# Packing and decoding sums on VectorE, a second tile for masked scores, and a planner that knows of a shared port

## The chip, the cores and the metric

The kernel runs on one core of one Trainium2 chip. Such a core has TensorE (PE: matrix products, and PEld: its weight loads), VectorE (DVE), ScalarE (ACT), GpSimd (POOL), and SyncE (SP), whose queue issues the kernel's DMA transfers. The metric is the device time of one execution in microseconds (us); lower is better. Before the change three runs gave 865.68, 868.64 and 872.82 us.

## The reference

What is computed is a recurrent attention with a state of 40 x 40 per head, followed by a gated product of two projections:

```python
# r, k, v, w, a, b: batch 4, heads 8, sequence 768, head_dim 40, float32
for t in range(S):
    y[:, :, t] = np.einsum('bhd,bhde->bhe', rt, state)
    Sa = np.einsum('bhde,bhe->bhd', state, at)
    state_decay = state * wt[:, :, None, :] - np.einsum('bhd,bhe->bhde', Sa, bt)
    state = state_decay + np.einsum('bhd,bhe->bhde', vt, kt)
x = y.transpose(0, 2, 1, 3).reshape(B * S, H * D)      # 3072 x 320
out = ((x @ w_a) * (x @ w_b)) @ w_out                  # d_ff = 1536
```

The three weights arrive in 64-bit floating point (a float32 array times a 64-bit scalar), everything else in float32.

## The kernel before

**Tiling.** The sequence is cut into 12 chunks of 64 tokens (n = 0 to 11). Each chunk has two halves of the heads (c = 0, 1), counted together as q = 2n + c, 24 in all. The inner dimension of 1536 is cut into 12 tiles of 128 (f). One *unit* is one tile for one chunk, so there are 144 units.

**Stages of a chunk.** `prep` loads W, BK and A of one q, forms cumulative products with two scans on VectorE (Q and pe), scales BK and A, multiplies them on TensorE into scores, writes one half of the scores to AB and the other, masked, to TK, and stores its results to un_d in DRAM. The rings of W, BK, A, Q and pe have two tiles, TK has one. `lanes` takes a pair of chunks (`GROUPS`): it transposes AB into N, runs 31 steps of two VectorE operations each (Yt, then Y), which invert small triangular matrices, and transposes the result into TC and T3 (the trace calls T3 "T"). `merge` makes the full inverse T from these; for all chunks but the first it copies TC into T by DMA (T<-TC). `main` is the part in which a chunk waits for the one before: the solve (u), the state (s), the outputs (G, y, X). `pack` reads the outputs back as XF, rounds them to a high part xk on ScalarE, and subtracts to get the low part on GpSimd.

**Units.** `decode` turns one piece of 64-bit weights (120 x 384, or 128 x 320 for the output weights) into a high and a low float32 part: five operations on VectorE, some copies on ScalarE, and at last a subtraction (into w_mt) and a sum (into wt or wo) on GpSimd. Three pieces make one tile. A unit multiplies xk by two tiles of wt into ab, forms g = a * b on VectorE and its rounded part gh on ScalarE, subtracts on GpSimd to get gl, and multiplies gh and gl by wo into po. Five tiles (F1) are decoded early and serve chunk 0 to 10 while the recurrence runs; the other seven are decoded at the end of it and during the tail, in which the stored xk of all chunks are read back.

**What sets the order.** All work is given to a planner (`Plan`) as operations with an engine, an estimated duration, dependencies and a priority `v`. `Plan.run` goes through the engines in simulated time: on each it takes, among the operations that can start within 0.05 us of the earliest, the one with the smallest `v`. The code is then emitted in this order, and each engine and the SP queue run their part in order. The priorities are built from PV and PV1 (preparation), LV and LV0 (lanes; LV0 for the first pair), MV (merge), UV (units), WV and WV1 (the first five weight tiles):

```python
prep(n, c, rank[n] + PV + PV1 * (n - rank[n]) + 0.1 * c)
lanes(g, g[0] + LV if g[0] else LV0)
wv = [WV + WV1 * f if f < F1 else NS - 3 + 0.3 * (f - F1) for f in range(NSL)]
```

Nearly all instructions go through a helper in line 68, so that the trace is read by the names of the tiles and not by lines.

Of the kernel before, what the change touches and what calls it, by code (L numbers as in the profile page):

```python
# [9 lines left out]
F32 = mybir.dt.float32  # L10
# [11 lines left out]
D = 40  # L22
C = 64
HB = 32
NP = 2
M = 8
# [47 lines left out]
class Op:  # L74
    __slots__ = ("eng", "dur", "fn", "deps", "users", "v", "lat", "need", "free", "mode", "end", "left", "ready", "seq", "moved", "work")

# [31 lines left out]
class Plan:  # L108
# [8 lines left out]

    def op(self, eng, dur, fn, r=(), w=(), v=None, lat=0.07, need=None, free=(), mode=None, moved=0.0, work=0):
        o = Op()
        o.moved, o.work = moved, work  # L120
# [29 lines left out]
    def run(self, slack=0.05, switch=0.13):  # L150
        engines = {e: 0.0 for e in ("PE", "DVE", "ACT", "POOL", "SP", "-")}
        ring = 0.0
        busy = dict.fromkeys(engines, 0.0)
        last_mode = None
# [10 lines left out]
        while todo:  # L165
            best = None
            for e, ops in ready.items():
                if not ops:
                    continue
                c = []  # L170
                for o in ops:
                    s = max(engines[e], o.ready)
                    if o.need:
                        bk = self.banks(o.need.n, s)
                        if bk is None:
                            continue
# [18 lines left out]
            if o.eng == "PE":  # L195
# [110 lines left out]
def wkv_moe(ctx, tc, wd, ai, bk, rvf, vn, pin, rv, wa, wb, wo, out):  # L306
# [86 lines left out]
    def decode(i, src, rows, ncol, dst_hi, dst_lo, split):  # L393
# [10 lines left out]
        if not WIDE:  # L404
# [53 lines left out]
    def plan_tile(f, w, slot, v):  # L458
        for i, j, (eng, dur, fn, r, wr, lat) in tile_steps(f, w):
# [15 lines left out]
    def unit(xk, kx, w, slot, first, last, done, v):  # L475
# [13 lines left out]
        for j in range(2):  # L489
# [81 lines left out]
    def prep(n, c, v):  # L571
# [12 lines left out]
        pl.op("DVE", us(2 * CW), lambda: nc.vector.tensor_tensor_scan(  # L584
            out=Q[:, CW::-1], data0=W[:, CW::-1], data1=one[:, ::-1], initial=0.0, op0=ALU.mult, op1=ALU.add), [kW], [kQ])
# [6 lines left out]
        eng, dur, te = ("POOL", gp, nc.gpsimd) if n >= ON_POOL else ("DVE", us, nc.vector)  # L592
        pl.op(eng, dur(2 * M * C), lambda: te.tensor_mul(
            out=BK, in0=BK,
            in1=Q[:, 2:2 + CW].rearrange("p (m t) -> p m t", t=CP)[:, :, None, 0:C].to_broadcast([P, M, 2, C])), [kQ], [kBK])
        pl.op("DVE", 0.41, rp, [kQ], ["d1"])

        pl.op("DVE", us(2 * CW), lambda: nc.vector.tensor_tensor_scan(
            out=PEt.rearrange("p m t -> p (m t)"), data0=W[:, 0:CW], data1=D1.rearrange("p m t -> p (m t)"),
            initial=0.0, op0=ALU.mult, op1=ALU.add), [kW, "d1"], [kPE])  # L600
        pl.op(eng, dur(M * C), lambda: te.tensor_mul(out=A, in0=A, in1=PEt[:, :, 0:C]), [kPE], [kA])
        pl.op("ACT", 0.18, lambda: nc.scalar.copy(out=pcs[:, n, c], in_=Qv[:, :, 1]), [kQ], [("pcs", n, c)])
# [67 lines left out]

    def lanes(g, v):

# [13 lines left out]
        pl.op("POOL", 1.2, start, w=["Y"])  # L686
        for s in range(HB - 1):
            ni, w = s + 1, HB - 1 - s

            def step(s=s, ni=ni, w=w):  # L690
                o = Wt[:, 0:ni * w].rearrange("p (i t) -> p i t", i=ni)
                nc.vector.tensor_mul(
                    out=o, in0=Yt[:, 0:ni, s:s + 1].to_broadcast([P, ni, w]),
                    in1=Nt[:, s:s + 1, s + 1:].to_broadcast([P, ni, w]))
                y = Yt[:, 0:ni, s + 1:]
                nc.vector.tensor_sub(out=y, in0=y, in1=o)
            pl.op("DVE", 2 * us(ni * w) + 0.03, step, ["N"], ["Y"])
        pl.op("DVE", 1.95, lambda: nc.vector.transpose(
            out=TC.rearrange("p x m t -> p t (x m)"), in_=Yt.rearrange("p s t -> p t s")), ["Y"], [("TC", 0), ("TC", 1)])
        pl.op("DVE", 1.95, lambda: nc.vector.transpose(  # L700
            out=T3.rearrange("p x m s -> p s (x m)"), in_=Yt), ["Y"], [("T3", 0), ("T3", 1)])

    def merge(n, x, v):
# [56 lines left out]
    def main(n, c, v):  # L760
# [56 lines left out]
        if n < NS - 1:  # L817
# [11 lines left out]
            if n:  # L829
# [6 lines left out]
                out=sv, in0=sv if n else bank(ps)[:, 0:320].rearrange("p (i q d) -> p i q d", q=2, d=D), in1=pc),  # L836
                src + [("pcs", n + 1, c)], [kST], free=[] if n else [(ps, 0)])

# [50 lines left out]
    def pack(n, v):  # L889
# [73 lines left out]
    for g in groups_of_chunks:  # L963
        for n in g:
            prepare(n)
        lanes(g, g[0] + LV if g[0] else LV0)
        if g[0] == 0:
            for f in range(F1):
                plan_tile(f, slots[f], f, wv[f])
        for x, n in enumerate(g):  # L970
            merge(n, x, n + MV)
            prepare(n + 1)
# [3 lines left out]
            if n < NS - 1:  # L976
# [71 lines left out]
    def plan_lazy(f, v):  # L1048
# [12 lines left out]
        for k, (i, j, (eng, dur, fn, r, wr, lat)) in enumerate(tile_steps_at(f, slots[0], base)):  # L1061
# [4 lines left out]
            r = list(r) + ["early"]  # L1066
            pl.op(eng, dur, lambda k=k, steps=steps: steps()[k][2][2](), r, wr, v=v, **kw)
        pl.dma(lambda: fill_rows(slots[slot][0]), [("wt", slot, j) for j in range(2)], [("wf", slot)], 0.3, 1.6, v=v)
# [222 lines left out]
```

## Time and profile before

| | us |
|---|---|
| median of three runs | 868.64 |
| lowest, highest | 865.68, 872.82 |
| the profiled execution | 862.4 |
| its span (first to last instruction) | 860.7 |
| TensorE busy in the span | 705.7 |
| VectorE busy | 581.2 |
| ScalarE busy | 394.6 |
| GpSimd busy | 239.2 |
| mean granted TensorE clock | 0.929 |

The rows of the profile are read so: a group is an engine, an operation, the tiles written and read, the shape and the count, then the busy time in us and the mean of one in ns, then the idle time of the engine just before them with what ended it. A row of waits reads "waiting engine and tile <- what came last: us in total, times, longest". In a timeline the first two numbers are the start and the length in us.

### The profile page before, as it was taken

What the parts mean: (1) busy time and instruction counts of PE and PEld (TensorE: products, weight loads), DVE (VectorE), ACT (ScalarE), POOL (GpSimd) and SP (SyncE); (2) the same over time, 40 slices, a digit from 0 to 9 for tenths busy, and PEclk for the clock granted to TensorE, in tenths of its full rate; (3) what the DMA queues carried; (4) which work ended last, traced back from release to release, by engine and by line L of the source; (5) the groups of instructions that cost most, each with busy time, mean ns of one, the idle gap of its engine ahead of it and who ended that gap; (6) DMA issues with size and microseconds to landing.
All of it is one profiled execution on the core that took longest, in us unless ns stands there. A gap on an engine that the chain in (4) does not pass through costs nothing.

```text
span 860.7 us, 29218 instructions
## 1 busy us (share of the span) xinstructions
PE 705.7 (82%) x12539; PEld 659.9 (77%) x12539; DVE 581.2 (68%) x1121; ACT 394.6 (46%) x1027; POOL 239.2 (28%) x271
## 2 busy tenths in 40 slices
PE   4325666687997898888978889989969999999995
PEld 3324555576887787777867778878969999999995
DVE  8797789999996889687955782256438883223343
ACT  4516553576446644663554435555425542222221
POOL 3000122343321102312220212246526662222221
PEclk9999677669999999999989899999989999999998
DMA  7984788888676968985876566974982210000022
GB/s 245 311 296 123 232 289 240 213 251 259 200 224 192 326 240 267 238 319 190 252 191 212 178 190 177 280 209 124 251 196 64 66 38 1 1 2 1 1 92 97
DMA packets 102019, 156.58 MB, mean 182 GB/s; under 512 B 30250, under 2 KB 70250, under 8 KB 98810
## 3 DMA queue, kind: packets, MB, share of 16 engines
q1 hardware_dynamic: 101882, 154.64, 59.4%
q8 instruction: 100, 1.64, 0.8%
q14 instruction: 37, 0.30, 0.1%
HBM read 101.97 MB, written 48.78 MB: 175 GB/s over the span
## 4 chain that ended last, share of the span: by engine, by line
PE 42%; DVE 27%; DMA 17%; issue 6%; ACT 4%; SPq 2%; POOL 1%; DVEq 0%; ACTq 0%; POOLq 0%
PE ab L68 20%; PE at L68 12%; PE po L68 10%; DVE Yt L68 6%; DVE Y L68 6%; DMA BK<-in_bk_dram 3%; DMA xk<-xk_d 2%; DMA wraw<-in_wa_dram 2%; SPq L68 2%; DVE w_ex L68 2%; DMA W<-in_wd_dram 2%; DVE BK L68 2%; DVE G L68 2%; DMA SV<-in_vn_dram 2%; DVE Q L68 1%
## 5 line engine op out<-in xcount | busy, mean ns | idle before, releaser
L68 PE MATMUL ab<-xk,wt 120*128 120x256 f32 x2304 | 316.1, 290 | 1.8 <-DVE g L68 1.0
L68 PEld LDWEIGHTS ab<-xk,wt 120*128 120x128 f32 x2304 | 297.9, 196 | 4.4 <-DVE g L68 1.2
L68 POOL TENSOR_TENSOR gl<-g,gh 128x256 fp32r<-128x256 f32 x144 | 118.3, 823 | 394.1 <-ACT gh L68 370.6
L68 DVE TENSOR_TENSOR g<-ab,g 128x256 f32<-128x256 f32 x144 | 60.5, 421 | 174.3 <-ACT g L68 173.9
L68 PE MATMUL po<-wo,gh 128*128 128x320 f32 x576 | 156.5, 321 | 10.9 <-ACT gh L68 8.7
L68 ACT COPY g<-ab 128x256 f32<-128x256 f32 x144 | 53.4, 371 | 144.8 <-PE ab L68 140.4
L68 PEld LDWEIGHTS po<-wo,gh 128*128 128x128 f32 x576 | 104.8, 193 | 13.3 <-ACT gh L68 9.8
L68 PE MATMUL po<-wo,gl 128*128 128x320 f32 x288 | 93.4, 324 | 6.9 <-POOL gl L68 6.8
L68 ACT CAST gh<-g 128x256 fp32r<-128x256 f32 x144 | 58.2, 405 | 66.9 <-DVE g L68 64.5
L68 DVE TENSOR_TENSOR Y<-Y,Yt 128x31 f32<-128x31 f32 (+15 forms) x186 | 73.0, 393 | 6.4
L68 DVE TENSOR_TENSOR Yt<-Y,N 128x31 f32<-128x31 f32 (+15 forms) x186 | 73.7, 396 | 4.9
L68 PE MATMUL at<-SV,un 128*64 128x40 f32 (+1 forms) x1472 | 50.9, 230 | 25.2 <-DMA SV<-in_vn_dram 10.2
L68 PEld LDWEIGHTS at<-SV,un 128*64 128x64 f32 (+1 forms) x1472 | 45.0, 141 | 31.6 <-issue 17.4
L68 PE MATMUL at<-ident,BK 128*128 128x128 f32 x192 | 39.0, 364 | 36.7 <-ACT AB L68 16.3
L68 PEld LDWEIGHTS po<-wo,gl 128*128 128x128 f32 x288 | 55.7, 194 | 12.0 <-POOL gl L68 11.4
L68 PEld LDWEIGHTS at<-ident,BK 128*128 128x128 f32 x192 | 30.2, 187 | 40.5 <-ACT AB L68 21.0
L68 POOL TENSOR_TENSOR w_mt<-w_mt,wt 120x384 f32<-120x384 f32 x24 | 26.2, 1090 | 93.8 <-ACT wt L68 74.0
L68 PE MATMUL at<-A,BK 64*64 64x64 f32 x1536 | 36.2, 258 | 13.3 <-ACT bkn L68 6.3
L68 PEld LDWEIGHTS at<-A,BK 64*64 64x64 f32 x1536 | 32.3, 168 | 18.2 <-ACT bkn L68 8.8
L68 DVE TENSOR_TENSOR BK<-BK,Q 128x1024 f32<-128x1024 f32 x24 | 30.9, 1286 | 21.0 <-DMA BK<-in_bk_dram 20.8
L68 DVE TENSOR_TENSOR acc<-po,acc 128x320 f32<-128x320 f32 x96 | 42.4, 481 | 3.1 <-PE po L68 2.5
L68 POOL TENSOR_TENSOR xk<-XF,xk 120x512 fp32r<-120x512 f32 (+1 forms) x24 | 33.2, 1405 | 37.5 <-ACT xk L68 37.5
(87 smaller groups left out, 1100.6 us busy)
## 6 DMA issues: line engine op xcount, KB each, us to landing
un<-un_d SPq DMA_DIRECT2D x24, 1092.0 KB
BK<-in_bk_dram SPq DMA_DIRECT2D x24, 512.0 KB
rv<-in_rvf_dram SPq DMA_DIRECT2D x24, 512.0 KB
xk_d<-xk SPq DMA_DIRECT2D x11, 720.0 KB
xk<-xk_d SPq DMA_DIRECT2D x11, 720.0 KB
un_d<-bkn SPq DMA_DIRECT2D x24, 320.0 KB
SV<-in_vn_dram SPq DMA_DIRECT2D x24, 320.0 KB
W<-in_wd_dram SPq DMA_DIRECT2D x24, 260.5 KB
```

Source lines behind the costliest of these rows:

```text
L68: r = fn(*args, **kwargs)
```

## The change

1. **Packing.** With `PACK_DVE = 12` the two subtractions of `pack` run on VectorE for all 12 chunks, in place of GpSimd.
2. **Decoding.** With `DEC_DVE = 15` the last subtraction and the sum of `decode` run on VectorE for the pieces 0 to 14, the five early tiles. Later pieces stay on GpSimd.
3. **gl.** The unit's subtraction gets the same switch, but `GL_DVE = 0` leaves it on GpSimd for every unit.
4. **TK.** `NTK = 2` gives the masked scores a second tile.
5. **The planner.** An operation can now hold a port. A GpSimd operation (all but the clearing of Y) and a marked VectorE operation may not overlap in the planned order: either waits for the end of the other engine's last one. Marked are the lane steps, the scans and products of `prep`, decoding, packing, and one product of `main`.
6. **Priorities.** All nine numbers change, for instance PV from -2.5 to -3.09, LV0 from -2.6 to -0.99, WV from 1.0 to -1.
7. **Not in use.** A way to halve the lanes (`HALVED`, `join`) is added, and `HALVED = ()` leaves it out. `ON_POOL`, which was 99 and never reached, is removed.

```diff
-NTK, NBN = 1, 1
+NTK, NBN = 2, 1
-ON_POOL = 99
+GL_DVE, PACK_DVE, DEC_DVE = 0, 12, 15
+HALVED = ()
-PV, PV1, LV, MV, UV, WV, WV1 = -2.5, 0.4, -0.6, -0.2, 1.6, 1.0, 0.3
-LV0 = -2.6
+PV, PV1, LV, MV, UV, WV, WV1 = -3.09, 0.6, -0.62, -0.34, 1.28, -1, 0.88
+LV0 = -0.99
...
+        o.moved, o.work, o.port = moved, work, port or (eng == "POOL" and dur != 1.2)
...
+        port = {"DVE": 0.0, "POOL": 0.0}
...
                     s = max(engines[e], o.ready)
+                    if o.port:
+                        s = max(s, port["DVE" if e == "POOL" else "POOL"])
...
+            if o.port:
+                port[o.eng] = s + d
...
-        yield "POOL", us(ncol, 0.2, 0.0027), lambda: nc.gpsimd.tensor_sub(
+        eng, d, te = ("DVE", us(ncol), nc.vector) if i < DEC_DVE else ("POOL", us(ncol, 0.2, 0.0022), nc.gpsimd)
+        yield eng, d, lambda: te.tensor_sub(
             out=shaped(f), in0=shaped(f), in1=dst_hi.bitcast(F32)), (kd + (0,),), (K[1],), None
-        yield "POOL", us(ncol, 0.2, 0.0027), lambda: nc.gpsimd.tensor_add(
+        yield eng, d, lambda: te.tensor_add(
             out=dst_lo, in0=shaped(f), in1=shaped(rf)), (K[1], K[2]), (kd + (1,),), None
...
-        pl.op("POOL", 0.76, lambda: nc.gpsimd.tensor_sub(out=gl, in0=g, in1=gh.bitcast(F32)),
-              [("g", i), ("gh", i)], [("gl", i)], v=v - 0.4)
+        eng, d, te = ("DVE", 0.43, nc.vector) if nunit <= GL_DVE else ("POOL", 0.76, nc.gpsimd)
+        pl.op(eng, d, lambda: te.tensor_sub(out=gl, in0=g, in1=gh.bitcast(F32)),
+              [("g", i), ("gh", i)], [("gl", i)], v=v - 0.4, port=True)
...
-        pl.op("POOL", 1.3, lambda: nc.gpsimd.tensor_sub(out=xk[:, 3:5], in0=XF[:, 0:2], in1=xf[:, 0:2]), kf + [k + (0,)], [k + (1,)], v=v)
+        eng, d, te = ("DVE", 0.7, nc.vector) if n < PACK_DVE else ("POOL", 1.38, nc.gpsimd)
+        pl.op(eng, d, lambda: te.tensor_sub(out=xk[:, 3:5], in0=XF[:, 0:2], in1=xf[:, 0:2]), kf + [k + (0,)], [k + (1,)], v=v, port=True)
...
-        pl.op("POOL", 1.3, lambda: nc.gpsimd.tensor_sub(
-            out=xk[0:D, 2:6:3], in0=XF[0:D, 2:4], in1=xf[0:D, 2:6:3]), kf, [k + (2,)], v=v)
+        pl.op(eng, d, lambda: te.tensor_sub(
+            out=xk[0:D, 2:6:3], in0=XF[0:D, 2:4], in1=xf[0:D, 2:6:3]), kf, [k + (2,)], v=v, port=True)
```

**GpSimd, before the first units.** w_mt, wt and wo are pieces of the second weight tile, xk the packing of chunk 0, gl and Y the units' subtraction and the clearing for the next lanes. Before:

```order
L68 TENSOR_TENSOR w_mt0_167<-w_mt0_167,wt1_231 120x384
L68 TENSOR_TENSOR wt1_231<-w_mt0_167,w_rs0_168 120x384
L68 TENSOR_TENSOR w_mt0_167<-w_mt0_167,wo1_232 128x320
L68 TENSOR_TENSOR wo1_232<-w_mt0_167,w_rs0_168 128x320
L68 TENSOR_TENSOR xk0_220<-XF_219,xk0_220 120x512
L68 TENSOR_TENSOR xk0_220<-XF_219,xk0_220 40x2x256
L68 TENSOR_TENSOR gl0_173<-g0_169,gh0_171 128x256
L68 TENSOR_TENSOR gl1_174<-g1_170,gh1_172 128x256
```

and now, from the clearing for the second pair on:

```order
L70 MEMSET Y_198 128x1024
L70 MEMSET Y_198 128x32
L70 TENSOR_TENSOR gl0_173<-g0_169,gh0_171 128x256
L70 TENSOR_TENSOR gl1_174<-g1_170,gh1_172 128x256
L70 TENSOR_TENSOR gl0_173<-g0_169,gh0_171 128x256
```

Decoding and packing have left this queue; gl and the clearing of Y remain.

**VectorE, at the first pair's lanes.** N is the transposed AB, Yt and Y the lane steps, the names with w_ the decoding. Before:

```order
L68 SCALAR_TENSOR_TENSOR Q0_183<-W0_181,one_81 128x521
L68 TENSOR_TENSOR TK0_191<-at2_65,tri_84 128x512
L68 STREAM_TRANSPOSE N_196<-AB_195 128x32x32
L68 TENSOR_TENSOR Yt_198<-Y_197,N_196 128x31
L68 TENSOR_TENSOR Y_197<-Y_197,Yt_198 128x31
L68 TENSOR_TENSOR Yt_198<-Y_197,N_196 128x60
```

and now:

```order
L70 STREAM_TRANSPOSE N_197<-AB_196 128x32x32
L70 SCALAR_TENSOR_TENSOR w_ex0_166<-wraw1_165,w_ex0_166 120x384
L70 TENSOR_TENSOR BK0_187<-BK0_187,Q0_183 128x1024
L70 TENSOR_TENSOR A0_189<-A0_189,pe0_193 128x512
L70 TENSOR_TENSOR w_mt0_167<-w_ex0_166,w_mt0_167 120x384
L70 TENSOR_TENSOR w_rs0_168<-w_rs0_168,w_ex0_166 120x384
L70 TENSOR_SCALAR w_ex0_166<-wraw0_164 128x320
L70 TENSOR_TENSOR w_mt0_167<-w_mt0_167,wt0_230 120x384
L70 TENSOR_TENSOR wt0_230<-w_mt0_167,w_rs0_168 120x384
L70 TENSOR_TENSOR TK0_191<-at1_64,tri_84 128x512
```

The steps used to follow the transpose at once; four more operations of decoding stand after these rows before the first of them.

**SP, at the inverses of the third pair.** T0 and T1 are the copies for chunk 4 and 5, which wait for the lanes; un_d12 is what the preparation of q = 12 stores, and so on. Before:

```order
L68 DMA T0_204<-TC_199 32x16x32 x4
L68 DMA T1_205<-TC_199 32x16x32 x4
L68 DMA un_d12_143<-pe0_192 128x520
L68 DMA un_d12_143<-A0_189 64x2x256 x2
L68 DMA un_d12_143<-bkn0_194 128x640
L68 DMA xk_d3_98<-xk1_221 120x1536
L68 DMA BK0_187<-in_bk_dram 128x1024
L68 DMA W0_181<-in_wd_dram 128x521
```

and now:

```order
L70 DMA T0_205<-TC_200 32x16x32 x4
L70 DMA T1_206<-TC_200 32x16x32 x4
L70 DMA xk_d3_98<-xk1_222 120x1536
L70 DMA un_d14_145<-pe0_193 128x520
L70 DMA un_d14_145<-bkn0_195 128x640
L70 DMA un_d14_145<-A0_189 64x2x256 x2
L70 DMA BK0_187<-in_bk_dram 128x1024
L70 DMA W0_181<-in_wd_dram 128x521
```

The loads of W and BK behind the copies are those of q = 14 before, and of q = 16 now: two rounds of preparation have moved ahead of them.

More of the change, by code (lines that the diff above doesn't have):

```diff
@@ L24 @@
 HB = 32
+QB = 16
 NP = 2
@@ L74 @@
 class Op:
-    __slots__ = ("eng", "dur", "fn", "deps", "users", "v", "lat", "need", "free", "mode", "end", "left", "ready", "seq", "moved", "work")
+    __slots__ = ("eng", "dur", "fn", "deps", "users", "v", "lat", "need", "free", "mode", "end", "left", "ready", "seq", "moved", "work", "port")
 class Banks:
@@ L356, in wkv_moe @@
             base=0, channel_multiplier=-1)
+    if HALVED:
+        off = const.tile([P, HB], F32, name="off")
+        nc.gpsimd.memset(off, 0.0)
+        nc.gpsimd.memset(off[:, QB:], -1.0)
+        eye = const.tile([P, HB], F32R, name="eye")
+        for qd in range(4):
+            sl = off[qd * HB:(qd + 1) * HB, :]
+            nc.gpsimd.affine_select(
+                out=sl, in_=sl, pattern=[[0, HB]], compare_op=ALU.is_ge, fill=0.0,
+                base=QB - 1, channel_multiplier=-1)
+            nc.scalar.copy(out=eye[qd * HB:(qd + 1) * HB, :], in_=ident[qd * HB:(qd + 1) * HB, qd * HB:(qd + 1) * HB])
     bias = const.tile([P, 1], F32, name="bias")
@@ L669, in prep, with lanes @@
         pl.op("ACT", 1.6, size, [kPE, kQ], [kW], v=v + 0.5)
-    def lanes(g, v):
+    def lanes(g, v, halved):
         pl.v = v
@@ L686, in lanes, with step, part @@
         pl.op("POOL", 1.2, start, w=["Y"])
[L687 to L697, printed above, removed]
+        if halved:
+            off_ = [AB[:, x0 + x, :, 0:HB] for x in range(len(g))]
+            for x in range(len(g)):
+                pl.op("DVE", us(512), lambda x=x: nc.vector.tensor_mul(
+                    out=off_[x], in0=off_[x], in1=off[:, None, :].to_broadcast([P, NP * M, HB])),
+                    ["N"], [("EO", x0 + x)] + kab, port=True)
+            for s in range(QB - 1):
+                ni, w = s + 1, QB - 1 - s
+                def step(s=s, ni=ni, w=w):
+                    def part(t, i0, n, t0, w):
+                        a = t[:, i0:i0 + 1, t0:t0 + 1]
+                        return bass.AP(tensor=a.tensor, offset=a.offset, ap=[a.ap[0], [QB * HB + QB, 2], [HB, n], [1, w]])
+                    o = Wt[:, 0:2 * ni * w].rearrange("p (b i t) -> p b i t", b=2, i=ni)
+                    nc.vector.tensor_mul(
+                        out=o, in0=part(Yt, 0, ni, s, 1).to_broadcast([P, 2, ni, w]),
+                        in1=part(Nt, s, 1, s + 1, w).to_broadcast([P, 2, ni, w]))
+                    y = part(Yt, 0, ni, s + 1, w)
+                    nc.vector.tensor_sub(out=y, in0=y, in1=o)
+                pl.op("DVE", 2 * us(2 * ni * w) + 0.03, step, ["N"], ["Y"], port=True)
+        else:
+            for s in range(HB - 1):
+                ni, w = s + 1, HB - 1 - s
+                def step(s=s, ni=ni, w=w):
+                    o = Wt[:, 0:ni * w].rearrange("p (i t) -> p i t", i=ni)
+                    nc.vector.tensor_mul(
+                        out=o, in0=Yt[:, 0:ni, s:s + 1].to_broadcast([P, ni, w]),
+                        in1=Nt[:, s:s + 1, s + 1:].to_broadcast([P, ni, w]))
+                    y = Yt[:, 0:ni, s + 1:]
+                    nc.vector.tensor_sub(out=y, in0=y, in1=o)
+                pl.op("DVE", 2 * us(ni * w) + 0.03, step, ["N"], ["Y"], port=True)
@@ L701, in lanes, with join, xt, t3 @@
             out=T3.rearrange("p x m s -> p s (x m)"), in_=Yt), ["Y"], [("T3", 0), ("T3", 1)])
+    def join(n, x, v):
+        pl.v = v
+        EO, XT = AB[:, place[n]], W4
+        ps = Banks(1)
+        def xt(ps=ps):
+            mul(bank(ps).rearrange("p (m t) -> p m t", t=HB), fl, eye[:, None, :].to_broadcast([P, NP * M, HB]), True, False)
+            for cm in range(NP * M):
+                for q in range(4):
+                    r = slice(q * HB, (q + 1) * HB)
+                    mul(bank(ps)[r, cm * HB:(cm + 1) * HB], EO[r, cm, 0:HB], T3[r, x, cm], False, True)
+        pl.op("PE", 2.55, xt, [("EO", place[n]), ("T3", x)], [("j1", n), "W4"], need=ps, work=3072, mode="h", lat=0.1)
+        pl.op("ACT", act(512), lambda ps=ps: nc.scalar.copy(
+            out=XT, in_=bank(ps).rearrange("p (m t) -> p m t", t=HB)), [("j1", n)], ["W4"], free=[(ps, 0)])
+        ps, ps2 = Banks(1), Banks(1)
+        def t3(ps=ps):
+            for cm in range(NP * M):
+                for h in range(2):
+                    r = slice(C * h, C * h + HB)
+                    mul(bank(ps)[r, cm * HB:(cm + 1) * HB], TC[r, x, cm], XT[r, cm])
+        def tc_(ps=ps2):
+            for cm in range(NP * M):
+                for q in range(4):
+                    r = slice(q * HB, (q + 1) * HB)
+                    mul(bank(ps)[r, cm * HB:(cm + 1) * HB], XT[r, cm], TC[r, x, cm])
+        pl.op("PE", 1.15, t3, ["W4", ("TC", x)], [("j2", n), ("T3", x)], need=ps, work=1024, mode="h", lat=0.1)
+        def t3c(ps=ps):
+            for h in range(2):
+                r = slice(C * h, C * h + HB)
+                nc.scalar.copy(out=T3[r, x], in_=bank(ps)[r].rearrange("p (m t) -> p m t", t=HB))
+        pl.op("ACT", 2 * act(512), t3c, [("j2", n)], [("T3", x)], free=[(ps, 0)])
+        pl.op("PE", 2.3, tc_, ["W4", ("j2", n)], [("j3", n), ("TC", x)], need=ps2, work=2048, mode="h", lat=0.1)
+        pl.op("ACT", act(512), lambda ps=ps2: nc.scalar.copy(
+            out=TC[:, x], in_=bank(ps).rearrange("p (m t) -> p m t", t=HB)), [("j3", n)], [("TC", x)], free=[(ps2, 0)])
     def merge(n, x, v):
@@ L965, in wkv_moe @@
             prepare(n)
-        lanes(g, g[0] + LV if g[0] else LV0)
+        halved = groups_of_chunks.index(g) in HALVED
+        lanes(g, g[0] + LV if g[0] else LV0, halved)
         if g[0] == 0:
@@ L970, in wkv_moe @@
         for x, n in enumerate(g):
+            if halved:
+                join(n, x, n + MV)
             merge(n, x, n + MV)
@@ L1066, in plan_lazy @@
             r = list(r) + ["early"]
-            pl.op(eng, dur, lambda k=k, steps=steps: steps()[k][2][2](), r, wr, v=v, **kw)
+            pl.op(eng, dur, lambda k=k, steps=steps: steps()[k][2][2](), r, wr, v=v, port=eng == "DVE", **kw)
         pl.dma(lambda: fill_rows(slots[slot][0]), [("wt", slot, j) for j in range(2)], [("wf", slot)], 0.3, 1.6, v=v)
```

22 lines of the change are left out of this document (10 added, 12 removed).

## The prediction

> **What bounds the kernel now.** I read the page's busy shares and slices first, then the chain of waits, then a table of stages.
>
> ```profile
> span 860.7 us, 29218 instructions
> ...
> PE 705.7 (82%) x12539; PEld 659.9 (77%) x12539; DVE 581.2 (68%) x1121; ACT 394.6 (46%) x1027; POOL 239.2 (28%) x271
> ...
> PE   4325666687997898888978889989969999999995
> DVE  8797789999996889687955782256438883223343
> ...
> PE 42%; DVE 27%; DMA 17%; issue 6%; ACT 4%; SPq 2%; POOL 1%; DVEq 0%; ACTq 0%; POOLq 0%
> ```
>
> TensorE (PE) is full only in the right third. To the left VectorE (DVE) is the fuller engine, and the chain runs through both. The stages are cut where each pair of chunks has its triangular inverses ready, at the six transposes into T3 (called T in the trace):
>
> ```profile
> L68 DVE STREAM_TRANSPOSE T<-Y x6: 1969/1993/2071, 70.0 to 512.4; 128x1024 f32<-128x1024 f32 x6
> ...
> core 0: us, PE busy (x) PEld busy (x) DVE busy (x) ACT busy (x) POOL busy (x), PEclk, DMA share, GB/s
> 0.00:70.04 70.04, 24.60 (x425) 20.48 (x425) 58.54 (x112) 24.07 (x63) 10.03 (x23) 1.00 0.78 262
> 70.04:155.69 85.65, 56.84 (x1526) 51.02 (x1526) 71.07 (x139) 44.67 (x115) 14.92 (x15) 0.78 0.80 241
> 155.69:251.45 95.76, 79.04 (x1711) 71.25 (x1712) 90.33 (x166) 54.94 (x141) 33.95 (x34) 0.84 0.77 231
> 251.45:340.82 89.37, 76.77 (x1878) 69.40 (x1877) 73.45 (x135) 49.72 (x136) 15.52 (x16) 0.94 0.78 245
> 340.82:425.13 84.31, 73.61 (x1740) 66.36 (x1740) 66.80 (x130) 45.82 (x127) 17.84 (x16) 0.94 0.80 252
> 425.13:512.40 87.27, 70.83 (x1770) 64.51 (x1768) 60.80 (x119) 41.23 (x111) 16.09 (x15) 0.90 0.66 196
> 512.40:600.00 87.60, 79.34 (x1604) 74.74 (x1602) 40.04 (x75) 46.57 (x118) 32.60 (x34) 0.98 0.70 196
> 600.00:652.00 52.00, 44.86 (x336) 43.82 (x335) 24.57 (x46) 18.79 (x46) 22.93 (x27) 0.93 0.82 205
> 652.00:860.70 208.70, 199.82 (x1565) 198.36 (x1563) 95.58 (x209) 68.82 (x172) 75.34 (x93) 0.99 0.11 36
> ```
>
> Columns two to six are the stage's length and the busy times of PE, its weight loads, DVE, ACT and POOL. The reader is to see that the pace of the first three stages is VectorE's: 90.33 of 95.76 us in the third. In the next three neither engine is full (PE idles 12.6, 10.7 and 16.4 us, VectorE 15.9, 17.5 and 26.5): they wait for each other and for loads. From 512 us on the inverses are done. By the order of the instructions TensorE has 50 of 144 expert units behind it when it begins the last chunk's solve, before and after, so what follows is the same work. Whatever shifts 512.4 us shifts the end.
>
> **The work that moves.** To 512.4 us POOL ran these:
>
> ```profile
> L68 POOL TENSOR_TENSOR gl<-g,gh 128x256 fp32r<-128x256 f32 x40 | 37.9, 950 | 221.9 <-ACT gh L68 200.5 <-issue 19.8 <-DVE w_rs L68 1.6
> L68 POOL TENSOR_TENSOR xk<-XF,xk 120x512 fp32r<-120x512 f32 (+1 forms) x18 | 25.4, 1435 | 25.9 <-ACT xk L68 25.9
> L68 POOL TENSOR_TENSOR wt<-w_mt,w_rs 120x384 fp32r<-120x384 f32 x10 | 12.9, 1285 | 1.1 <-DVE w_rs L68 0.6
> L68 POOL TENSOR_TENSOR w_mt<-w_mt,wt 120x384 f32<-120x384 f32 x10 | 10.9, 1095 | 79.3 <-ACT wt L68 62.1 <-DVE Q L68 5.3 <-DVE Yt L68 4.4
> L68 POOL TENSOR_TENSOR wo<-w_mt,w_rs 128x320 fp32r<-128x320 f32 x5 | 4.5, 903 | 0.4
> L68 POOL TENSOR_TENSOR w_mt<-w_mt,wo 128x320 f32<-128x320 f32 x5 | 4.3, 864 | 28.7 <-ACT wo L68 28.7
> ```
>
> The gl row stays (GL_DVE is 0), and the halved lanes and `join` are not used (HALVED is empty). The 18 packing and 30 decoding subtractions and sums go to VectorE. Its price for such shapes (minimum/median/maximum, ns):
>
> ```profile
> L68 DVE TENSOR_TENSOR A<-A,pe x24: 653/689/1602, 7.8 to 455.5; 128x512 f32<-128x512 f32 x24
> ...
> L68 DVE TENSOR_TENSOR w_rs<-w_rs,w_ex x36: 475/548/2574, 40.4 to 706.0; 120x384 f32<-120x384 f32 x24, 128x320 f32<-128x320 f32 x12
> ...
> L68 DVE TENSOR_TENSOR_SCAN Q<-W,one x24: 1215/1243/2678, 3.8 to 433.7; 128x521 f32<-128x521 f32 x24
> ```
>
> 18 x 0.689 + 20 x 0.548 + 10 x 0.475 = 12.4 + 11.0 + 4.7 = **28.1 us more on VectorE**. The same rows show what comes back: maxima are two to five times the median. Such records have a POOL operation beside them (the columns are the start and the length in us):
>
> ```profile
> 90.29 2.04 DVE L68 TENSOR_TENSOR_SCAN Q<-W,one 128x521 f32<-128x521 f32 x1
> ...
> 139.86 0.42 DVE L68 TENSOR_TENSOR Y<-Y,Yt 128x247 f32<-128x247 f32 x1
> 140.31 1.50 DVE L68 TENSOR_TENSOR Yt<-Y,N 128x240 f32<-128x240 f32 x1
> 141.85 1.37 DVE L68 TENSOR_TENSOR Y<-Y,Yt 128x240 f32<-128x240 f32 x1
> ...
> 140.26 2.70 POOL L68 TENSOR_TENSOR xk<-XF,xk 120x512 fp32r<-120x512 f32 x2 [9.00 <-ACT xk L68]
> ...
> 490.61 1.40 DVE L68 TENSOR_TENSOR Y<-Y,Yt 128x256 f32<-128x256 f32 x1
> ```
>
> Two lane steps that should take 0.41 us take 1.50 and 1.37 while POOL packs. Between the 90.29 and the 490.61 record, 35 records of VectorE are longer than the usual one of their shape and lie mostly beside a packing or decoding operation; together they are 28.8 us too long. So **28.8 us come back**, and the two terms nearly cancel. Bounds of the return: 28.8 if the neighbour was the cause, nothing if others take its place. I take the whole, since each of the 35 has its operation beside it.
>
> The Trainium skill (SBUF — State Buffer, section "SBUF: two separate sides") has the port of these two engines as an exclusive lock, held for a whole instruction. By that rule the return is whole, as the rows have it; a port that was merely shared would return about half, 14.4 us, and the sum below would be 871.6.
>
> **Order and second TK tile.** The rest is in the order: new numbers for the priorities, and a planner that keeps the two engines apart. Three places matter.
>
> Loads for preparation. SP's queue runs in order, and the copy T<-TC waits there for the inverses. Before, 14 of the 24 loads of W and of BK stand ahead of it in the third pair; afterwards 16, and in the fifth 24 of each instead of 24 and 22. So the next pair's loads no longer begin behind that wait. What VectorE and TensorE wait for there, 250 to 600 us:
>
> ```profile
> DVE BK L68 <- DMA BK<-in_bk_dram: 11.0, 4, 4.9
> DVE Q L68 <- DMA W<-in_wd_dram: 6.5, 3, 2.9
> DVE TK L68 <- DMA un_d<-TK: 2.2, 1, 2.2
> ...
> PE po L68 <- POOL gl L68: 5.0, 7, 1.4
> ```
>
> 11.0 + 6.5 = 17.5 us could go; the other end is 0, because the queue's DMA share is 0.66 to 0.80 in those stages and a load moved ahead can hold up another. I take half, **8.7 us**. The second TK tile by itself is worth 0 to 2.2 us (one wait in the run) and is counted in that half: with it a pair's scores need not wait until the former TK has been stored.
>
> POOL's queue. A gl behind two packings waits some 2.8 us; TensorE waits 5.0 us for gl in seven places. Gain 0 to 5.0; I take **2**, since some of the seven are gl held by VectorE.
>
> The ramp. Between the transpose into N and the first lane step of the first pair VectorE now has 13 operations, ten of decoding and three of preparation: some 7.5 us, if the ten take the 0.475 to 0.548 of w_rs and the three the 0.689 to 1.243 of A and Q. Two of the weight loads also stand ahead of the fourth load of BK in SP's queue. All of this has to be done anyway, and the first weights are ready sooner: by the order three units instead of one stand before the third chunk's solve. TensorE idles 28.8 us in the second stage, where that can be used. Bounds +7.5 and -5; I take 0, as the two are alike in size.
>
> The tail from 600 us keeps its decoding on POOL (pieces 15 and up). One load of output weights slides behind the reloads of xk; it can repeat this stall once more, 0 to 6.3 us; I take 0, TensorE has a queue of units there.
>
> ```profile
> 642.79 0.63 PE L68 MATMUL po<-wo,gh 128*128 128x320 f32 x1 [6.31 <-ACT gh L68]
> ```
>
> **Sum.** The profiled execution took 862.4 us (span 860.7 and 1.7 around it). 862.4 + 28.1 - 28.8 - 8.7 - 2.0 = 851.0, a gain of 11.4 us. The median of the runs, 868.64, lies 6.2 us above that execution; carried over to it: 868.6 - 11.4 = **857.2 us**.
>
> **Rivals.**
> *More than that:* the waits of the fourth to sixth stage go and TensorE sets the pace. It idles 39.7 us there; half of it, 19.9, and the 2 of gl make 846.7. For it: VectorE's 59.9 idle us there. Against it: the waits lie on several releasers, and a solve, a state and the next solve depend on each other.
> *The order does nothing:* the loads are paced by their rings of two and by the DMA share, and come as late as now. Then only 0.7 and 2.0 go: 865.9. For it the share of 0.8 in the early stages, against it the loads that now stand ahead of the wait.
> *Slower, by a packing that heads VectorE's queue:* on POOL a packing may wait for its rows at no cost (25.9 us in the row above). On VectorE all lane steps queue behind it, and TensorE's next solve behind them. The copy ahead of it waits for its rows:
>
> ```profile
> ACT xk L68 <- DMA XF<-x_d: 7.5, 6, 2.6
> ```
>
> 7.5 us is the least by which packings would be late, 25.9 the most by these rows. With 25.9 the time is 857.2 + 25.9 = 883.1. It decides from 20.1 us on, where the time passes 877.3. Against it: the planner sets the packing where it expects the rows.
> *Slower, by a full VectorE:* nothing of the 28.8 comes back, because lanes now meet gl where they met packings. 857.2 + 28.8 = 886.0. For it gl's 40 operations of 950 ns that stay, against it the 35 records with another neighbour. The Trainium skill (Perfetto Trace Analysis, section "Optimizing Scalar/DVE Operations") would hand work from a saturated VectorE to others, the reverse of this change, and adds that between these two engines that may not help, for the port.
>
> **How the numbers follow.** About 1% (8.7 us) is what a measurement of this kernel tells from no change. Forecast 0.45, with a range of its own of 848 to 866, two thirds of it under 860; more than that 0.15; the order does nothing 0.18; the packing in front 0.14; a full VectorE 0.08. Faster by over 1%: 0.30 + 0.15 = 0.45. Within 1%: 0.15 + 0.18 = 0.33. Slower: 0.22. The forecast's own range is its sum with the loads' term at 0 and at 17.5. The range goes from 843, which leaves out a third of the larger gain, to 882, which leaves out the upper half of both slower cases: 0.05 and 0.11.
>
> **What would show it.** Right: VectorE's scans and lane steps near their medians wherever POOL runs no gl; VectorE's busy time to the last T3 within 5 us of 421; waits for BK and W after 250 us under 9 us; the last T3 at 495 to 508 us. Wrong: idle time of VectorE ahead of xk operations (packing in front), gl rising above 1.1 us with lane steps lengthened as often as now (full VectorE), or the last T3 at 512 with waits for BK and W as long as before (the order does nothing).

## The result and the profile after

| kernel | median of its runs | kernel before beside it | ratio, 95% interval |
|---|---|---|---|
| changed, first time | 837.8 us (4 runs, 834.5 to 844.5) | 869.3 us (4 runs) | 0.9648 [0.9575, 0.9720] |
| changed, measured again | 840.3 us (6 runs, 836.2 to 852.5) | 864.7 us (17 runs, 856.6 to 880.4) | 0.9728 [0.9676, 0.9779] |

Medians are of all runs of a kernel, while a ratio compares only the runs within 1.5% of the fastest of their kernel, so it need not be the quotient of two medians.

The change is faster by 24 to 31 us. The prediction said faster, with 857.2 us and a range that began at 843. It was right in direction, but the time is 17 to 19 us below its forecast and 3 to 5 us below its range, and the gain of 11.4 us that it named is less than half of the measured one.

The first profile of the changed kernel is its slowest run (844.5 us, span 842.8). The readings below are from the second one (836.2 us, span 834.5), which lies 4 us below its median, as the profile of before (862.4) lies 2 to 7 us below its own. The page of that second profile, busy shares, slices and chain:

```profile
span 834.5 us, 29196 instructions
...
PE 691.6 (83%) x12539; PEld 651.0 (78%) x12539; DVE 569.3 (68%) x1175; ACT 396.7 (48%) x1027; POOL 167.0 (20%) x217
...
PE   4332758658899888988897999979979999999996
...
DVE  8789888898989767887886884266347765232343
...
PE 53%; DMA 17%; DVE 8%; ACT 6%; issue 4%; SPq 1%; POOL 1%; ACTq 0%; DVEq 0%; POOLq 0%
```

VectorE (DVE) fell from 27% of the chain to 8%, TensorE (PE) rose from 42% to 53%. TensorE's idle time, span less busy time, went from 155.0 to 142.9 us, and its busy time from 705.7 to 691.6 for the same 12539 products. So more than half of the 26.2 us between these two spans is shorter busy time, and why the same products took less was not tried. The stages, cut as before at the six transposes into T3:

```profile
L70 DVE STREAM_TRANSPOSE T<-Y x6: 1852/1988/2020, 75.7 to 502.1; 128x1024 f32<-128x1024 f32 x6
```

(in the first profile they run from 75.8 to 508.8 us)

```profile
0.00:75.74 75.74, 23.23 (x425) 19.88 (x425) 61.82 (x124) 25.62 (x63) 7.17 (x21) 0.61 0.78 249
75.74:172.43 96.69, 64.95 (x1658) 58.13 (x1658) 83.92 (x173) 54.73 (x140) 3.76 (x5) 0.75 0.80 253
172.43:265.91 93.48, 80.23 (x1794) 73.35 (x1795) 83.40 (x173) 53.74 (x140) 9.53 (x12) 0.86 0.77 242
265.91:353.30 87.39, 75.92 (x1812) 69.99 (x1811) 66.72 (x133) 46.58 (x127) 10.60 (x13) 0.90 0.78 244
353.30:431.32 78.02, 68.62 (x1801) 62.77 (x1800) 64.76 (x131) 46.10 (x125) 8.31 (x11) 1.00 0.84 268
431.32:502.12 70.80, 63.50 (x1610) 58.17 (x1609) 55.92 (x117) 37.72 (x103) 8.03 (x11) 0.95 0.68 207
502.12:590.00 87.88, 82.83 (x1634) 77.32 (x1633) 43.09 (x89) 47.71 (x122) 28.46 (x33) 1.00 0.76 214
590.00:642.00 52.00, 47.31 (x363) 47.10 (x362) 26.87 (x57) 21.50 (x52) 22.31 (x28) 0.97 0.64 161
642.00:834.50 192.50, 185.00 (x1455) 184.28 (x1454) 82.79 (x188) 62.98 (x156) 68.86 (x85) 0.99 0.10 34
```

The second stage is 11 us longer than it was (96.69 against 85.65), the fifth 6 us and the sixth 16 us shorter. The last T3 comes 10.3 us sooner, at 502.1 instead of 512.4, and **what follows it takes 332.4 us instead of 348.3**. In the last three rows TensorE is busy for 315.1 us with 3452 products, where it was 324.0 us with 3505, and idle for 17.2 us instead of 24.3. In the first profile the last T3 comes 3.6 us sooner and what follows takes 334.0 us. The stages end at other amounts of work, though, so they do not say alone where time was gained. For that the next rows cut both kernels where TensorE had done equal work, each product weighted by the mean time of its group; their numbers in brackets are nearly the same. First the kernel before:

```profile
413.88:546.67 132.79, 114.00 (x2756) 104.44 (x2754) 81.77 (x162) 63.42 (x171) 24.08 (x25) 0.94 0.70 207
546.67:673.33 126.66, 112.51 (x1322) 108.63 (x1320) 72.47 (x136) 59.68 (x145) 61.57 (x67) 0.96 0.67 174
```

Then the changed kernel:

```profile
410.60:528.20 117.60, 109.74 (x2779) 101.22 (x2776) 85.71 (x182) 63.18 (x173) 13.95 (x19) 0.97 0.73 224
528.20:648.50 120.30, 111.12 (x1321) 107.41 (x1322) 62.87 (x133) 57.14 (x139) 51.30 (x59) 0.99 0.68 185
```

259.5 us became 237.9: **21.6 of the 26.2 us between the two spans lie in this stretch**. TensorE idles 17.0 us there instead of 32.9, and its busy time is 5.7 us less, with a granted clock of 0.97 and 0.99 instead of 0.94 and 0.96. Up to 413.9 us only 3.3 us had been gained, and the tail from 648.5 us takes 186.0 us against 187.4.

The waits of VectorE on loads and of TensorE on gl, 250 to 600 us:

```profile
DVE Q L70 <- DMA W<-in_wd_dram: 5.4, 2, 3.2
...
DVE BK L70 <- DMA BK<-in_bk_dram: 2.2, 2, 1.3
```

```profile
PE po L70 <- POOL gl L70: 1.1, 3, 0.5
```

17.5 us of waits for W and BK became 7.6, 5.0 us for gl became 1.1, and the 2.2 us for the store of TK are gone. How far such sums vary by themselves is seen in experiment 9.

### The profile page after: what moved, and what is told of

It is laid out like the page before. It is cut to its first block, busy times and chain, and to the rows that moved or that the text cites. A ratio compares the mean times of both kernels' runs of the same rounds, so it can differ in the third digit from the quotient of the medians.

```text
span 842.8 us, 29196 instructions
## 1 busy us (share of the span) xinstructions
PE 690.6 (82%) x12539; PEld 650.2 (77%) x12539; DVE 570.4 (68%) x1175; ACT 396.2 (47%) x1027; POOL 167.4 (20%) x217
## 4 chain that ended last, share of the span: by engine, by line
PE 53%; DMA 22%; DVE 10%; ACT 6%; issue 5%; SPq 2%; POOL 1%; ACTq 0%; DVEq 0%; POOLq 0%
PE ab L70 25%; PE at L70 16%; PE po L70 12%; DMA SV<-in_vn_dram 6%; DMA XF<-x_d 3%; DMA x_d<-X 3%; DMA wraw<-in_wo_dram 2%; DVE Yt L70 2%; DVE Y L70 2%; DMA acc<-po_d 2%; SPq L70 2%; DMA wraw<-in_wa_dram 2%; DMA un_d<-A 2%; ACT SV L70 1%; DMA un_d<-bkn 1%
## 5 line engine op out<-in xcount | busy, mean ns | idle before, releaser
L70 PE MATMUL ab<-xk,wt 120*128 120x256 f32 x2304 | 311.3, 288 | 9.1 <-DVE g L70 8.3
L70 PEld LDWEIGHTS ab<-xk,wt 120*128 120x128 f32 x2304 | 294.5, 194 | 12.6 <-DVE g L70 8.7
L70 POOL TENSOR_TENSOR gl<-g,gh 128x256 fp32r<-128x256 f32 x144 | 113.9, 793 | 537.6 <-ACT gh L70 535.0
L70 DVE TENSOR_TENSOR Y<-Y,Yt 128x31 f32<-128x31 f32 (+15 forms) x186 | 65.4, 352 | 6.4
L70 DVE TENSOR_TENSOR Yt<-Y,N 128x31 f32<-128x31 f32 (+15 forms) x186 | 64.6, 347 | 4.6
L70 PE MATMUL at<-ident,BK 128*128 128x128 f32 x192 | 33.7, 324 | 19.2 <-DVE TK L70 7.0
L70 ACT COPY SV<-ST 64x160 f32<-64x160 f32 x88 | 28.5, 323 | 37.6 <-DMA SV<-in_vn_dram 35.1
L70 PEld LDWEIGHTS at<-ident,BK 128*128 128x128 f32 x192 | 25.7, 165 | 22.8 <-DVE TK L70 7.9
L70 ACT COPY SV<-at 64x160 f32<-64x160 f32 x96 | 27.5, 287 | 25.3 <-PE at L70 24.0
L70 PE MATMUL at<-T,AB 32*32 32x32 f32 x768 | 17.0, 204 | 25.3 <-DVE T L70 23.1
```

What stands on the lines that cost most here:

```text
L70: r = fn(*args, **kwargs)
```

## The experiments

Each ratio is to runs of the kernel before on the same chip. "Old order" is that of the kernel before and "new order" that of the changed one, instruction by instruction on every engine.

### 1. The sums on VectorE, the old order

```diff
-lambda: nc.gpsimd.tensor_sub(out=shaped(f), ...)
+lambda: (nc.vector if i < 15 else nc.gpsimd).tensor_sub(out=shaped(f), ...)
...
-lambda: nc.gpsimd.tensor_sub(out=xk[:, 3:5], ...)
+lambda: nc.vector.tensor_sub(out=xk[:, 3:5], ...)
```

(and the same for the sum of decoding and the second subtraction of packing)

> The order of the kernel before, with nothing changed in its planner or numbers; only the packing of all pairs of chunks and the decoding sums of pieces 0 to 14 are issued on VectorE instead of GpSimd (POOL), at the places where the old order has them relative to their inputs. Placement theory (the gain lies in where the sums run, because a POOL operation holds up VectorE): 838 to 850 us, and the records of VectorE to the last T3 fall back to their medians. Order theory (the sums cancel, 28.1 against 28.8, and the numbers and the port in the planner make the gain): 862 to 875 us. If the sums, at places planned for POOL, head VectorE's queue: above 875 us.

870.4 us (10 runs), ratio 0.9993 [0.9943, 1.0044]: no change. VectorE to the last T3 at 513.5 us, in a row of windows, and its moved groups there:

```profile
0.00:513.50 513.50, 384.72 (x9042) 345.68 (x9042) 416.16 (x843) 260.51 (x693) 47.33 (x71) 0.89 0.76 235
```

```profile
L68 DVE TENSOR_TENSOR xk<-XF,xk 120x512 fp32r<-120x512 f32 (+1 forms) x18 | 12.7, 706 | 7.1 <-ACT xk L68 7.0
...
L68 DVE TENSOR_TENSOR w_mt<-w_mt,wt 120x384 f32<-120x384 f32 x10 | 5.4, 543 | 0.7 <-ACT wt L68 0.7
L68 DVE TENSOR_TENSOR wt<-w_mt,w_rs 120x384 fp32r<-120x384 f32 x10 | 5.4, 542 | 0.0
...
L68 DVE TENSOR_TENSOR w_mt<-w_mt,wo 128x320 f32<-128x320 f32 x5 | 2.4, 482 | 0.9 <-ACT wo L68 0.9
L68 DVE TENSOR_TENSOR wo<-w_mt,w_rs 128x320 fp32r<-128x320 f32 x5 | 2.4, 480 | 0.0
```

The five groups add 28.3 us, yet VectorE's busy time fell from 421.0 to 416.2, so 33.1 us came back. Counted record by record up to the last T3, those more than 0.25 us over the median of their shape were 53 in the kernel before, 37.4 us too long together, and are 20 here, 9.1 us too long. The 20 lie beside gl or the clearing of Y, which stay on GpSimd. That is what the placement theory wanted to see, and still the time stood. In the old order placement alone is not the gain.

### 2. The sums on POOL, the new order

```diff
-eng, d, lambda: te.tensor_sub(out=shaped(f), ...)
+eng, d, lambda: nc.gpsimd.tensor_sub(out=shaped(f), ...)
```

(and the same for the other three)

> The changed kernel's order, but the packing and the decoding sums are issued on POOL at the same places. Placement theory: the lengthened records of VectorE come back beside them, 855 to 875 us. Order theory: the sums cancel here too, 832 to 846 us. A mixture would lie between, 846 to 855 us.

845.0 us (4 runs), ratio 0.9750 [0.9676, 0.9825], within the order theory's numbers. Against 0.9648 and 0.9728 the sums' place would be worth 0.2 to 1.0% here, 2 to 9 us, but the interval holds 0.9728, so that it is worth anything by itself is not shown.

### 3 and 4. The priority numbers

```diff
-PV, PV1, LV, MV, UV, WV, WV1 = -3.09, 0.6, -0.62, -0.34, 1.28, -1, 0.88
-LV0 = -0.99
+PV, PV1, LV, MV, UV, WV, WV1 = -2.5, 0.4, -0.6, -0.2, 1.6, 1.0, 0.3
+LV0 = -2.6
```

The first of the two is the changed kernel with this edit, the second the kernel before with its reverse. (The numbers are eight, as the diff has them; the texts on record speak of nine.)

> The changed kernel with the nine old priority numbers; the placement of the sums, the port in the planner and the second TK tile stay as changed. If the numbers make the gain: 860 to 875 us. If placement and port make it: 832 to 848 us. If the numbers were merely fitted to the placement, so that neither stands alone: 848 to 860 us.

> The kernel before with the nine new priority numbers and nothing else. If the numbers make the gain: 832 to 848 us. If placement and port make it: 862 to 880 us, since the numbers then only shift work whose limits stay as they were.

866.4 us, ratio 1.0013 [0.9964, 1.0062], and 862.0 us, ratio 0.9947 [0.9898, 0.9995]. The old numbers lose the whole gain, and the new ones alone bring 0.5%. Each result by itself points at the other half, so neither half alone makes the gain. The second kernel also speaks on a premise of the prediction; its row is shown with that of the next.

### 5. The planner without the port

```diff
-o.moved, o.work, o.port = moved, work, port or (eng == "POOL" and dur != 1.2)
+o.moved, o.work, o.port = moved, work, False
```

> The changed kernel, its planner no longer keeping VectorE and POOL apart; the sums stay on VectorE. If keeping them apart makes the gain: 850 to 870 us, with records of VectorE lengthened beside gl. If the lengthened records are not what costs (the sums already left POOL, only gl and the tail's decoding remain there): 835 to 845 us.

858.4 us, ratio 0.9880 [0.9802, 0.9958]: 1.5 to 2.3% lost. The records of VectorE beside gl did lengthen, as the first theory has it, but by little: 21 records up to the last T3 are more than 0.25 us over the median of their shape, 9.5 us together, where the changed kernel has 10 and 4.7 us. So most of the 13 to 20 us lies in the other order that the planner makes. The last T3 of experiment 4, and of this kernel:

```profile
L68 DVE STREAM_TRANSPOSE T<-Y x6: 1874/1982/2047, 74.8 to 495.4; 128x1024 f32<-128x1024 f32 x6
```

```profile
0.00:491.13 491.13, 365.92 (x8753) 331.85 (x8753) 414.04 (x833) 256.84 (x677) 47.17 (x71) 0.90 0.77 241
```

The second row is the window up to that kernel's last T3. The two reach it at 495.4 and 491.1 us, before the changed kernel (502.1 and 508.8), and end later (spans 857.4 and 856.1). In the latter TensorE has 8753 products behind it at that point, in the six stages of the changed kernel some 9100, so 365.0 us follow where the changed kernel has 332.4. So the last T3 by itself doesn't set the end. What TensorE has done by then counts as much.

### 6. Rounded numbers

```diff
-PV, PV1, LV, MV, UV, WV, WV1 = -3.09, 0.6, -0.62, -0.34, 1.28, -1, 0.88
-LV0 = -0.99
+PV, PV1, LV, MV, UV, WV, WV1 = -3.0, 0.6, -0.6, -0.3, 1.3, -1, 0.9
+LV0 = -1.0
```

> The changed kernel with its nine numbers rounded to one digit (-3.0, 0.6, -0.6, -0.3, 1.3, -1, 0.9 and -1.0). If the numbers express a sound order of priorities, rounding costs nothing: 834 to 842 us. If the gain belongs to one order that was found among many, it is partly lost: 845 to 868 us.

848.0 us, ratio 0.9811 [0.9708, 0.9913]. The small edit gives another order, which keeps 1.9% of the 2.7 to 3.5%. The interval holds 0.9728, so the loss is likely but not clear of noise.

### 7 and 8. One TK tile: planned, and in the new order

The first kernel has `NTK, NBN = 1, 1`, and the planner makes another order. The second keeps the new order and lets both tiles be one:

```diff
-TK_[q % NTK]
+TK_[0]
```

> The changed kernel with one TK tile instead of two; the planner makes another order for it. If the second tile itself carries the gain: 855 to 870 us, with waits for TK and its store ahead of the scores. If it is worth what the prediction gave it (0 to 2.2 us): 836 to 841 us. If the gain belongs to this one order, which any change of the planner's input breaks up: anything from 838 to 870 us without longer waits for TK.

> The changed kernel with every engine's order as it is, but the two TK tiles are one and the same, so that scores may have to wait until the former TK has been stored. If the second tile is worth little by itself, as the prediction has it (0 to 2.2 us): 836 to 842 us. If it carries the gain, with the order following from it: 850 to 870 us.

870.4 us, ratio 0.9978 [0.9920, 1.0036], and 850.6 us, ratio 0.9829 [0.9775, 0.9883]. The first kernel's other order loses everything, with 4.9 us of waits for TK's store in two places, and so can't price the tile. In the new order, with nothing else changed, the tile is worth 1.0 to 1.8%, 9 to 16 us. Its four runs (849.8 to 852.3 us) lie above five of the six runs of the changed kernel beside them (836.2 to 846.4; the sixth took 852.5). The view of TK in the second kernel: what VectorE waited for ahead of the masked scores, and who waited for these:

```profile
L70 DVE TENSOR_TENSOR TK<-at,tri x24: 652/684/692, 11.0 to 466.5; 128x512 f32<-128x512 f32 x24
its engine sat idle before it (us, times) until:
  DMA un_d<-TK: 30.1, 7
...
  PE at L70: 31.7, 9
```

30.1 us in seven waits, where the kernel before had 2.2 in one. The cause is in the starts of these records. The last two of the kernel before, then those of the changed one (first profile):

```profile
453.35 0.69 DVE L68 TENSOR_TENSOR TK<-at,tri 128x512 f32<-128x512 f32 x1
464.59 0.69 DVE L68 TENSOR_TENSOR TK<-at,tri 128x512 f32<-128x512 f32 x1 [2.21 <-DMA un_d<-TK]
```

```profile
455.24 0.68 DVE L70 TENSOR_TENSOR TK<-at,tri 128x512 f32<-128x512 f32 x1
456.16 0.69 DVE L70 TENSOR_TENSOR TK<-at,tri 128x512 f32<-128x512 f32 x1 [0.24 <-ACT AB L70]
```

They are 11.2 us apart before and 0.9 us after. That pair is the extreme: of the 23 distances between starts, five are 0.9 to 6.4 us in the changed kernel, and the shortest of the kernel before is 7.0. The new order puts the scores of some halves closer together than one tile, busy until its store is done, allows. With one tile the same five are 8.6 to 11.1 us.

### 9. The second TK tile in the old order

```diff
-TK_ = ring(pp, NTK, [P, 2, 4, C], "TK")
+TK_ = ring(pp, 2, [P, 2, 4, C], "TK")
-TK_[q % NTK]
+TK_[q % 2]
```

> The kernel before with two TK tiles and every engine's order to the last solve as it is. If the second tile helps whatever the order: 854 to 860 us, as it was worth about 10 us in the new order. If it pays only where the order runs ahead enough to need it (the trace of before has one wait of 2.2 us for TK's store): 863 to 869 us.

866.5 us, ratio 0.9987 [0.9946, 1.0027]: nothing, as the old order's one wait has it. In its trace VectorE waits 11.4 us for W and 13.2 us for BK between 250 and 600 us, 24.6 in all, where the kernel before has 17.5 in the same order. So these waits can differ by 7 us while the time stays.

### 10. The loads behind the copies, the new order

The planner's order is kept; ahead of the issue the last six loads of W, BK and A that stand before the first T<-TC of the third and the fifth pair are taken out and put behind it.

```diff
...
+for name, k in (("diag4", 6), ("diag8", 6)):
+    i = next(j for j, o in enumerate(ops) if o.tag == name)
+    for j in [j for j in range(i) if ops[j].tag == "load"][-k:][::-1]:
...
+        ops.insert(i, ops.pop(j))
+        i -= 1
```

> The changed kernel's order with only SP's queue changed: in the third and the fifth pair of chunks the last six loads of W, BK and A that stand ahead of the copies T<-TC are issued directly behind the first of these copies. If these loads being ahead of that wait is worth the 8.7 us of the prediction: 843 to 856 us, with VectorE's waits for BK and W back at 11 to 20 us between 250 and 600 us. If the loads were never what held the stages: 836 to 841 us.

859.6 us (4 runs, 848.0 to 864.8), ratio 0.9814 [0.9702, 0.9926]: by the ratios 0.9 to 1.7% are lost, 7 to 14 us. But this ratio rests on two of the four runs (848.0 and 856.5), and its interval holds 0.9728, so the loss is not clear of noise. The median lies above both ranges that were expected. The profile is of a third run (862.7 us), so the waits that come back are read from experiment 12, in which the same loads are moved.

### 11. The copies off SP's queue, the old order

```diff
-nc.sync.dma_start(out=T[r, :, HB * k:HB * k + HB], in_=TC[r, x])
+nc.scalar.dma_start(out=T[r, :, HB * k:HB * k + HB], in_=TC[r, x])
```

> The kernel before, with the copies T<-TC issued from ScalarE's queue instead of SP's; nothing else moves. Then no load of the next pair waits behind the inverses in SP's queue. If that wait is what the old order pays for the loads: 850 to 860 us, with VectorE's waits for BK and W between 250 and 600 us under 9 us. If the loads come late in the old order because their buffers are not free yet: 863 to 872 us. If ScalarE, waiting for the inverses, holds up its other copies: above 872 us.

871.2 us, ratio 1.0071 [1.0030, 1.0112]: no gain, but 0.3 to 1.1% lost. VectorE still waits for BK (11.0 us before):

```profile
DVE BK L68 <- DMA BK<-in_bk_dram: 9.2, 3, 5.2
```

Its wait for W, 6.5 us before, is no longer in the list, so the two together are 9.2 us instead of 17.5. That fits copies that held W in SP's queue, while most of BK's wait has another cause, but one trace doesn't show it where such waits differ by 7 us by themselves (experiment 9). No gain came of it. That ScalarE's other work paid for it, as the third theory has it, isn't excluded: ScalarE now waits for the copies in three places, 11.1 us in all, and the time is up.

### 12. All three taken back, the new order

The edits of experiments 2, 8 and 10 together.

> The changed kernel's order with three things taken back together: the sums on POOL, the six loads of the third and of the fifth pair behind the copies T<-TC, and one TK tile. If these three hold the whole gain: 863 to 880 us. If more of it lies elsewhere in the order: 845 to 858 us.

865.6 us (10 runs), ratio 0.9994 [0.9955, 1.0033]. The whole gain is gone, with every other instruction in the new order. VectorE's waits for the loads, 250 to 600 us, and the transposes into T3:

```profile
DVE Q L70 <- DMA W<-in_wd_dram: 10.7, 3, 4.7
...
DVE BK L70 <- DMA BK<-in_bk_dram: 4.1, 4, 2.5
```

```profile
L70 DVE STREAM_TRANSPOSE T<-Y x6: 1928/1977/2042, 76.2 to 524.9; 128x1024 f32<-128x1024 f32 x6
```

The waits are 14.8 us instead of 7.6. The last T3 comes 12.5 us later than in the kernel before (512.4), yet what follows it takes 331.7 us (span 856.6), as in the changed kernel and not 348.3 as before. So the new order by itself shortens what follows the last T3 by 16 to 17 us and pays for it ahead of the last T3, and the second tile, the loads and the sums' place together win that price back.

### 13. The halved lanes

```diff
-HALVED = ()
+HALVED = (0, 1, 2, 3, 4, 5)
```

> The changed kernel with the halved lanes and the join on TensorE, which the change brings but does not use, for all six pairs. VectorE has 15 lane steps instead of 31 for each pair, TensorE some 5 products more. If VectorE's lanes still set the pace of the first stages: 815 to 835 us. If the order and the serial solves set it, or if the new order that the planner makes loses what the present one has: 838 to 875 us.

931.6 us, ratio 1.0760 [1.0696, 1.0825]. Neither theory's numbers hold: it is much slower. From its page:

```profile
PE 778.3 (84%) x16391; PEld 728.5 (78%) x16391; DVE 500.9 (54%) x995; ACT 423.9 (46%) x1079; POOL 170.6 (18%) x223
```

VectorE is 68 us lighter and TensorE has 3852 more products and 87 us more to do, in a kernel that TensorE ends. The expectation had put TensorE's part at some five products. No version beat the changed kernel.

## Why the prediction was too small

**"Whatever shifts 512.4 us shifts the end", since what follows is the same work: wrong, and this is the step that failed.** Up to the last T3 the sum nearly holds: 10.3 us sooner in the second profile, where it has 11.4. What follows the last T3 stands in the sum at nothing, and it took 332.4 us instead of 348.3, 15.9 us less (3.6 and 14.3 in the first profile). TensorE now has more of its units behind it at the last T3, 42 instead of 40, and it idles less afterwards. The count of 50 units holds for the start of the last chunk's solve, which comes later, and not for the last T3. All signs that were named for "right" came: VectorE's records too long only beside gl, its 416.5 us, 7.6 us of waits, a last T3 at 502.1 us (508.8 in the first profile is just outside). The time still fell outside the range, because these signs look no further than the last T3 or the waits of VectorE.

The step is not wrong everywhere. In five profiles in the new order (the changed kernel twice, experiments 2, 8 and 12) 331.7 to 335.4 us follow the last T3, though it comes at 502 to 525 us, so within one order a shift of it does shift the end. It doesn't from one order to another: the last T3 of experiments 4 and 5 comes at 495.4 and 491.1 us, and 362.0 and 365.0 us follow. These kernels ended 13 us and more behind one with 508.8 us. The rival "more than that" did count TensorE's idle time and came nearest, with 846.7 us, in part by luck: it took half of 39.7 us in the fourth to sixth stage, and there 11.5 went. Over equal work from 413.9 us on, 15.9 of 32.9 went.

**Plus 28.1 for the moved sums: right.** Experiment 1 has 28.3. **Minus 28.8 that come back: right.** There the excess of the records that were too long fell by 28.3 us (37.4 to 9.1), and VectorE's busy time without the moved work by 33.1. Its busy time to the last T3 is 416.5 us in the changed kernel (the sum of the first six rows above), within the 5 us of 421 that were named. The two terms cancel as worked out, and in the old order they are worth nothing (0.9993). The exclusive lock of the Trainium skill (SBUF — State Buffer, section "SBUF: two separate sides") wants a whole return. The trace agrees, with 28.3 us of the 28.8. It is the lock's time that comes back, though, not the kernel's.

**The second TK tile, 0 to 2.2 us: wrong.** It is worth 9 to 16 us in the new order. The price was read from the waits of the old order, in which the tile is hardly ever short. A buffer's worth has to be read in the order that uses it: the new order puts two scores 0.9 us apart, and the listing of that order, without any time in it, shows these two as neighbours.

**Minus 8.7 for the loads: right size of wait, its worth not shown.** The waits fell by 9.9 us (17.5 to 7.6), and stood under the 9 that were named; with the loads back behind the copies they are 14.8 us in experiment 12. What that costs by itself, 7 to 14 us in experiment 10, is not clear of noise. In the old order experiment 11 nearly halves the same waits without a gain, and experiment 9 lengthens them by 7 us without a loss.

**Minus 2 for gl: right in sign, a bit small.** The waits fell by 3.9 us.

**The ramp, 0 within -5 and +7.5: held by TensorE's work.** That of the first 413.9 us is done 3.3 us sooner in the second profile and 4 to 5 us later in the first. By the transposes the second and the third T3 come 16.7 and 14.5 us later than before, and only the sixth sooner.

**The sum as a sum: wrong.** Its 11.4 us lie near the 10.3 by luck, since the tile was priced too low and the price of the new order ahead of the last T3, 12.5 us in experiment 12, was not in it. The terms also depend on the order. Alone in the old order the sums, the priority numbers and the second tile gave ratios of 0.9993, 0.9947 and 0.9987; in the new order the tile is worth up to 16 us, the loads and the sums' place perhaps up to 14 and 9, and without the three the rest is worth nothing (0.9994). The planner's order is made for all of them. How the gain divides among them can't be settled: taken back one by one they cost 18 to 39 us in all by the ratios, taken back together the 24 to 31 that there are. The three together in the old order were not tried.

**The carry to the median: fair.** The profiles of before and of the changed kernel measured again both lie a little under their medians and differ by 26.2 us, the medians beside each other by 24.4, and by 31.5 the first time.

Of the rivals on the slower side neither came. VectorE's waits for the copy ahead of packing were 7.5 us between 250 and 600, far from the 20.1 from which that case decides:

```profile
DVE xk L70 <- ACT xk L70: 7.5, 8, 2.9
```

## What to carry to other kernels

Where an order is planned, price a buffer, a queue's order and an operation's engine together in the new order and not one by one in the old trace, since a wait that the old order never runs into has no row there. Find the engine that sets the end and count its idle time over equal amounts of its work; an event on another engine tells of the end only as long as the same work follows it. A gain that hangs on an order can show next to nothing when its parts are tried singly in the old kernel, so take them back singly, and together, from the new one.

## What the runs showed of the hardware

The executions of the kernel before spread more than expected: 856.6 to 880.4 us in 17 runs of one sitting, so that a single profile can lie 1 to 2% from the median. From 410 us on the changed kernel had the higher granted clock (0.97 and 0.99 against 0.94 and 0.96) with less idle time of TensorE; how the two hang together was not tried. The granted clock up to the first T3 is recorded as 1.00 in the profile of before and as 0.61 in that of the changed kernel, but the same 425 products took 24.60 and 23.23 us there. So the recorded clock of that stretch, and with it the mean of a whole run (0.929 and 0.901), does not tell how fast the products ran.

A VectorE operation beside a subtraction or a sum on GpSimd took up to 2.6 us where it usually takes 0.55 (the row of w_rs in the prediction), and with these sums gone from GpSimd, in experiment 1, no record of its first 513.5 us was more than 0.25 us over the median of its shape but beside gl and the clearing of Y.
